# A mixer block on one core: separate first loads, later zeroing, two more tiles finished by accumulating transfers, and a new step list

## The chip, the cores and the metric

The kernel runs on one core of a Trainium2 chip. The core's engines work side by side, each through its own instructions in order: TensorE (PE in the profile; its weight loads are listed as PEld), VectorE (DVE), ScalarE (ACT) and GpSimd (POOL). SyncE (SP) issues most DMA transfers here; ScalarE and POOL issue some as well. The metric is the time of one execution in microseconds (us) on the device. For the kernel before it is 189.82 us, the median of three runs (189.74 to 190.06).

## The reference

The input x has 2048 rows of 512 bfloat16 numbers. After a layer norm, two branches run on the same normalised rows xn: a local attention with 32 heads of 16 numbers, eight positions per row at a distance of 2 (branch A), and a small mixer with two dense stages (branch B). The output is x + A * silu(B).

```python
def _A_ref(x, wqkv, wo):
    q, k, v = ...                    # x @ wqkv, 32 heads of 16
    idx = pos[:, None] - off[None, :]      # off = 0, 2, ..., 14
    logits = jnp.einsum("bhsd,bhswd->bhsw", q, kg) * scale
    logits = jnp.where(mask[None, None, :, :], logits, -1e9)
    attn = _softmax(logits, axis=-1)
    o = jnp.einsum("bhsw,bhswd->bhsd", attn, vg)
    return o @ wo                    # heads put side by side again

def _B_ref(x, w1, w2, w3, w4):
    h = _gelu(_layernorm(x, axis=-1) @ w1)
    # four quarters of h, shifted by +1, -1, +2, -2 rows, then @ w2
    x1 = x + hs
    h2 = _gelu(_layernorm(x1, axis=-1) @ w3) @ w4
    return x1 + h2

xn = _layernorm(x, axis=-1)
s = _A_ref(xn, A_wqkv, A_wo)
g = _silu(_B_ref(xn, B_w1, B_w2, B_w3, B_w4))
return x + s * g
```

## The kernel before

The 2048 rows are four chunks of 512, and a chunk is four tiles of 128 rows, so the tiles are numbered 0 to 15. Row p*4 + i of a chunk stands in partition p of the chunk's tile i. All is computed in bfloat16 with sums in float32.

The kernel is written as some seventy small functions, the steps, each of which emits a few instructions for a tile or a chunk. A long text, ORDER, lists the steps with their arguments, and the instructions of each engine stand in exactly that order: `w1.5.3` is the step w1 for tile 5 with its sums in bank 3. Nothing else schedules the work. An instruction waits where it needs another's result; everything behind it on its engine waits with it. That holds for the transfers that SP issues, too.

The steps that matter here, with the lines of the kernel before:

- Loads. `ldxp` (L221) loads two tiles of x, 256 KB; `ldxc` (L211) a whole chunk; `ldv`, `ldw1`, `ldqk` and others the weights. All are issued on SP.
- Constants. `c_warm` clears a tile for the warm-up products (`warmup`, L321), which multiply zeros while the first loads are under way. `c_elog` and `c_sel` build selection matrices on POOL. `c_zero` (L288 to L290) stores 14 rows of zeros ahead of the rows of v in DRAM, and clears the edges of hT.
- First norm. For chunk 0, `st` (L333) takes the statistics of a tile on VectorE, `sq0` (L338) a root on ScalarE, `nm0` (L345) scales the tile, `tr0` (L356) turns it with four transposes on TensorE, and `ev0h` or `ev0a` take it from PSUM to xnT. Later chunks are turned by DMA (`xT`).
- Products of xn: `v` (L471), with `ev` and `sv` (L489) that store v to DRAM; `qk` (L443); `w1` (L496), with `eh` and the transpose `hTr` (L515).
- Attention: `pw` (L530) multiplies q with k shifted by each of the eight offsets, `lg` (L543) adds up the 16 numbers of a head with 32-column products, softmax follows, `vl` (L710) reads the eight rows of v for a tile from DRAM, `vp` (L716) weights them, `ws` (L729) adds them up on TensorE with 32-column products, `eo` evacuates. The sums are turned by DMA (`oTr`, L748), for the last chunk by TensorE (`oTp`, L756) with `eoT` (L762) on ScalarE to evacuate. `wo` (L768) is the last product of branch A.
- Branch B: `w2` (L611), `xa`, `st3s`, `nm3`, `x1Tr` (L655), `w3` (L668), `eg` (L677), `w4` (L685), `ya` (L692), `si` (L696).
- The end of a tile. For tiles 0 to 11, `sg` (L775) multiplies the sum of `wo` with silu(B) on VectorE, straight from PSUM. The rows of x were copied to the output earlier, from DRAM to DRAM (`pre`, L828, one for each of three chunks), and `soa` (L835) adds the product to them: a transfer with accumulation, issued on POOL. For tiles 12 to 14, `ge` (L782) evacuates the sum on ScalarE, `gb` (L786) multiplies, `fav` (L819) adds x on VectorE, and `so` (L839) stores the tile, on SP for 13 and 14 and on ScalarE's queue for 12. Tile 15 goes in two halves: `woh` (L793), `sgh` (L802), `favh` (L807), `soh` (L813), the first half stored on SP and the second on ScalarE's queue.

Of the kernel before, what the change touches and what calls it, by code (L numbers as in the profile page):

```python
# [22 lines left out]
qk.0.4.1 qk.0.5.5 nmv.6 nmv.7 st.11 ldxc.s.3 st.10 st.8 eqk.0.3 eqk.0.5 qk.0.2.2 eqk.0.0
qk.0.6.4 eqk.0.2 st.9 eqk.0.4 qk.0.7.3 eqk.0.6 eqk.0.7 pw.0.1 rp.5 st.15 st.13 rp.4 xT.3 hTr.0
ldw2.s hTr.1 w1.4.1 v.5.4 ldwo.s.0 ev.5 w1.5.3 v.4.2 ev.4 qk.1.4.4 rs.4 sv.4 v.6.5 w1.7.2 rr.3
rr.2 eh.4 pw.0.2 kh.1 ev.6 sv.5 rs.5 nb.4 pw.0.0 st.12 eqk.1.4 eh.5 w1.6.1 qk.1.1.4 qk.1.2.3
v.7.5 hTr.2 nm.8 nm.9 w2.1.0 pw.0.3 nb.5 rp.6 eh.6 xT.4 vl.s.1.1 eh.7 st.14 rp.7 lg.0.0 rs.7
eqk.1.2 lg.0.1 ev.7 pw.0.5 w2.0.5 rs.6 eqk.1.1 nm.11 nm.10 pw.0.4 sv.7 qk.1.5.4 sv.6 xT.5
qk.1.6.3 xa.1 nb.7 qk.1.0.2 nb.6 st3s.1 eqk.1.6 hTr.3 rr.4 xa.0 ldw3.s.0 st3s.0 eqk.1.5 pw.0.6
nm.13 nm.12 nm.15 qk.1.7.0 qk.1.3.4 w2.2.5 w1.9.3 w1.8.1 eh.9 eh.8 xa.2 rr.7 hTr.4 rr.5 rq.0  # L30
w1.10.5 pw.0.7 r3.0 v.8.3 eh.10 st3s.2 nm.14 w2.3.1 nm3.0 nm3.1 eqk.1.3 w2.5.5 ev.8 qk.2.0.4
xa.3 st3s.3 eqk.1.7 eqk.1.0 xT.6 lg.0.3 rq.1 kh.2 xa.5 lg.0.2 r3.1 w2.4.2 smx.0 ldw3.s.1 sv.8
xT.7 x1Tr.0 v.10.5 qk.2.4.0 w2.6.1 eqk.2.4 nm3.3 xa.4 ex.0 w2.7.3 w1.11.2 xa.6 st3s.6 nm3.2 xa.7
qk.2.5.1 eqk.2.0 x1Tr.1 eh.11 ev.10 sv.10 rr.6 v.9.0 v.11.3 w1.13.4 eqk.2.5 ev.9 hTr.5 qk.2.7.2
w1.15.1 eqk.2.7 w1.12.0 vl.s.2.0 vl.s.0.0 ldw4.s.2 qk.2.2.2 vl.s.3.1 eh.12 pw.1.0 st3s.4 st3s.7
st3s.5 v.12.5 eqk.2.2 pw.1.3 sms.0 eh.13 v.13.0 w3.0.6.4 ev.11 hTr.6 rq.2 qk.2.1.3 pw.1.2 r3.2
sv.9 eg.0.6 eqk.2.1 ldwo.s.3 smn.0 rq.3 pw.1.1 r3.3 w3.0.1.2 qk.2.3.4 w3.0.10.3 nm3.4 eqk.2.3
tE.0 eh.15 eg.0.10 ev.13 eg.0.1 lg.1.1 lg.1.0 pw.1.7 w2.8.1 w1.14.0 w3.0.0.2 eh.14 w3.0.2.3
hTr.7 qk.2.6.0 eqk.2.6 eg.0.0 w2.10.4 nm3.6 vl.s.0.1 nm3.7 x1Tr.3 vl.s.1.0 pw.1.5 xa.8 pw.1.4
nm3.5 pw.1.6 w2.11.1 xa.10 w3.0.8.2 xa.11 qk.3.1.4 st3s.11 eg.0.8 ev.12 w2.14.1 lg.1.2 st3s.10  # L40
sv.12 lg.1.3 eqk.3.1 w2.12.4 sv.11 st3s.8 eg.0.2 smx.1 w2.9.3 ldw4.s.1 x1Tr.2 xa.9 w2.15.5 xa.14
w3.0.3.2 w3.0.9.3 xa.12 pw.2.2 qk.3.2.1 qk.3.0.4 w2.13.0 st3s.9 eqk.3.2 eqk.3.0 eg.0.3 vl.s.9.1
ldw4.s.0 rq.4 xa.15 vl.s.9.0 vl.s.3.0 ldwo.s.2 pre.s.2 qk.3.3.1 w3.0.5.2 st3s.12 qk.3.4.5 eg.0.5
pw.2.3 eqk.3.3 qk.3.5.4 st3s.14 pw.2.4 xa.13 pw.2.1 rq.5 st3s.15 v.15.1 eqk.3.5 v.14.2 ev.15
eqk.3.4 w3.1.1.0 w3.0.4.5 vp.0 st3s.13 rq.6 pw.2.0 r3.4 nm3.9 w3.0.7.1 eg.0.4 ev.14 eg.0.9
eg.0.7 ex.1 qk.3.7.4 w3.1.0.2 eg.1.0 sv.14 r3.5 nm3.10 rq.7 nm3.11 x1Tr.5 w3.1.8.1 vl.s.2.1
pre.s.1 vl.s.10.0 vl.s.10.1 w4.1.3 eqk.3.7 ldwo.s.1 kh.3 sv.15 r3.7 c_sel sms.1 w4.0.5 w4.2.4
ya.0 smn.1 r3.6 w3.1.5.5 w4.3.2 nm3.8 ya.2 ya.1 vp.1 x1Tr.4 w3.1.9.3 nm3.15 eg.1.5 ya.3 w3.1.6.4
pre.s.0 vp.3 tE.1 w3.1.7.2 eg.1.6 eg.1.1 w3.1.3.5 w3.1.4.0 eg.1.7 vp.2 lg.2.1 lg.2.0 qk.3.6.2
eg.1.8 w3.1.10.1 eqk.3.6 nm3.14 pw.2.5 pw.2.7 w3.1.2.4 eg.1.3 eg.1.10 eg.1.4 lg.2.2 pw.2.6  # L50
x1Tr.7 eg.1.2 ws.2.1 ws.1.0 ws.0.4 eg.1.9 pw.3.2 ws.3.3 eo.1 lg.2.3 eo.0 smx.2 vl.s.4.1 w4.6.0
w3.2.0.4 oTr.0 eo.2 eo.3 oTr.1 vl.s.5.1 pw.3.0 ex.2 vl.s.4.0 vl.s.6.0 vl.s.5.0 w4.5.3 vl.s.6.1
ya.6 pw.3.4 w4.7.0 w4.4.1 w3.2.3.5 sms.2 si.2 si.1 si.3 eg.2.0 eg.2.3 si.6 vl.s.7.1 vl.s.7.0
pw.3.1 pw.3.5 nm3.12 ya.4 wo.1.4 nm3.13 ya.7 w3.2.2.1 sg.1 w3.2.9.0 vp.4 ya.5 w3.2.5.4 w3.2.4.5
eg.2.9 w3.2.1.2 smn.2 x1Tr.6 w3.2.8.0 vp.5 eg.2.4 eg.2.2 eg.2.5 w3.2.10.1 w3.2.7.4 w3.2.6.5
eg.2.7 eg.2.10 eg.2.1 eg.2.8 vp.6 tE.2 vl.s.8.1 vl.s.8.0 wo.0.3 eg.2.6 wo.2.1 wo.3.0 pw.3.3 sg.2
w4.10.5 soa.2 sv.13 sg.3 vp.7 w3.3.0.0 lg.3.0 eg.3.0 lg.3.2 si.4 pw.3.6 pw.3.7 ws.4.0 ws.5.1
lg.3.1 ws.7.2 ws.6.4 eo.4 ya.10 lg.3.3 vl.s.11.1 w4.9.0 smx.3 eo.5 si.7 si.0 eo.7 si.5 eo.6
si.10 vl.s.13.1 oTr.2 vl.s.13.0 vl.s.11.0 w4.8.2 vp.9 vl.s.12.1 ex.3 oTr.3 w4.11.4 ya.8 ya.9
sms.3 ya.11 smn.3 w3.3.7.0 w3.3.5.2 w3.3.1.5 eg.3.5 vp.10 tE.3 wo.4.4 eg.3.7 eg.3.1 vl.s.14.1  # L60
vl.s.12.0 sg.0 vl.s.14.0 vp.11 w3.3.4.1 w3.3.9.2 w3.3.10.5 eg.3.10 w3.3.8.0 w3.3.3.3 w3.3.6.5
eg.3.9 eg.3.4 vp.8 w3.3.2.1 eg.3.6 eg.3.8 wo.6.2 eg.3.2 eg.3.3 wo.7.0 sg.6 vp.13 ws.10.3 ws.9.2
eo.10 ws.11.1 ws.8.5 eo.9 w4.13.3 vl.s.15.0 sg.4 vl.s.15.1 vp.12 eo.11 eo.8 wo.5.4 si.11 oTr.5
vp.14 si.9 w4.12.5 oTr.4 w4.15.1 ya.12 sg.5 si.12 si.8 sg.7 vp.15 w4.14.0 soa.1 soa.0 soa.3
# [810 lines left out]
```

## Time and profile before

| | |
|---|---|
| median of the unprofiled runs | 189.82 us |
| the profiled execution | 190.75 us |
| its span, first to last instruction | 189.0 us |
| mean granted TensorE clock | 0.996 |
| TensorE busy | 182.8 us |
| VectorE busy | 165.1 us |
| ScalarE busy | 112.8 us |
| POOL busy | 42.7 us |
| DMA queue of SP, share of 16 engines | 74.6% |
| DMA queue of POOL, share of 16 engines | 10.9% |

The span is measured on the profiled execution from the first to the last instruction, and all moments below count from its start. The profiled execution itself takes 1.75 us more than its span. In the profile, a group of instructions is named by its line and by what it writes and reads (`xr<-mm,xr`); `mm` stands for a bank of PSUM. A matmul's duration there (0.379 us for 512 columns) is longer than the distance from one to the next, since they are pipelined. In the chain of waits the profile goes back from the last instruction, at each step to whatever released it. `xc` is the tile of x, `w2v_sb` holds the weights w2 and wv, `vt` the evacuated sums.

### The profile page before, as it was taken

What the parts mean: (1) busy time and instruction counts of PE and PEld (TensorE: products, weight loads), DVE (VectorE), ACT (ScalarE), POOL (GpSimd) and SP (SyncE); (2) the same over time, 40 slices, a digit from 0 to 9 for tenths busy, and PEclk for the clock granted to TensorE, in tenths of its full rate; (3) what the DMA queues carried; (4) which work ended last, traced back from release to release, by engine and by line L of the source; (5) the groups of instructions that cost most, each with busy time, mean ns of one, the idle gap of its engine ahead of it and who ended that gap; (6) DMA issues with size and microseconds to landing.
All of it is one profiled execution on the core that took longest, in us unless ns stands there. A gap on an engine that the chain in (4) does not pass through costs nothing.

```text
span 189.0 us, 3685 instructions
## 1 busy us (share of the span) xinstructions
PE 182.8 (97%) x1430; PEld 87.0 (46%) x1430; DVE 165.1 (87%) x270; ACT 112.8 (60%) x189; POOL 42.7 (23%) x70
## 2 busy tenths in 40 slices
PE   7999999999999999999999999999999999999990
...
GB/s 164 315 352 115 199 248 141 194 238 137 233 120 286 278 64 224 222 87 190 399 162 361 274 57 134 254 401 277 189 190 95 254 335 238 210 254 106 88 106 116
DMA packets 47842, 39.25 MB, mean 208 GB/s; under 512 B 35251, under 2 KB 41889, under 8 KB 47777
## 3 DMA queue, kind: packets, MB, share of 16 engines
q1 hardware_dynamic: 45008, 35.14, 74.6%
q0 software_dynamic: 2528, 3.69, 10.9%
q8 instruction: 11, 0.18, 0.4%
q10 hardware_dynamic: 288, 0.20, 0.3%
q14 instruction: 7, 0.05, 0.1%
...
## 4 chain that ended last, share of the span: by engine, by line
PE 85%; DMA 4%; DVE 4%; issue 2%; POOL 2%; SPq 1%; ACT 1%; POOLq 0%
PE mm L668 20%; PE mm L685 18%; PE mm L443 15%; PE mm L611 8%; PE mm L496 7%; PE mm L471 6%; PE lg L543 4%; PE mm L768 4%; DMA xc<-in_A_x_dram 3%; PE mm L729 3%; POOL out_dram L835 2%; DMA out_dram<-xr 1%; DVE st L333 1%; DVE xr L775 1%; DVE xr L786 1%
## 5 line engine op out<-in xcount | busy, mean ns | idle before, releaser
L530 DVE TENSOR_TENSOR pw<-qT,kT 128x2048 bf16<-128x2048 bf16 x32 | 38.3, 1214 | 3.4 <-PE lg L543 2.4
L668 PE MATMUL mm<-x1T,w_sb 128*128 128x512 bf16 (+1 forms) x176 | 40.9, 379 | 0.0
L685 PE MATMUL mm<-w_sb,h 128*128 128x512 bf16 (+1 forms) x176 | 39.4, 379 | 0.0
L677 ACT ACTIVATE h<-mm 128x512 bf16<-128x512 f32 (+1 forms) x44 | 23.9, 602 | 23.3 <-PE mm L668 17.6
L716 DVE TENSOR_TENSOR vs<-vs,att 128x4096 bf16<-128x4096 bf16 x16 | 36.2, 2285 | 0.0
L443 PE MATMUL mm<-xnT,wqk_sb 128*128 128x512 bf16 x128 | 30.6, 379 | 0.0
L835 POOL DMA_DIRECT2D out_dram<-xr x12 | 11.0, 1117 | 74.0 <-DVE xr L775 74.0
L668 PEld LDWEIGHTS <-w_sb 128*128 128x128 bf16 (+1 forms) x176 | 17.6, 100 | 20.4
L685 PEld LDWEIGHTS <-h 128*128 128x128 bf16 (+1 forms) x176 | 16.9, 98 | 20.8 <-issue 0.4
L443 PEld LDWEIGHTS <-wqk_sb 128*128 128x128 bf16 x128 | 12.4, 98 | 15.0
L452 ACT ACTIVATE kT<-mm 128x512 bf16<-128x512 f32 x16 | 9.4, 601 | 12.1 <-PE mm L443 11.9
L489 POOL DMA_DIRECT2D v_dram<-vt x16 | 9.6, 601 | 30.6 <-ACT vt L481 27.2
L471 PE MATMUL mm<-w2v_sb,xnT 128*128 128x512 bf16 x64 | 15.8, 379 | 0.0
L496 PE MATMUL mm<-w_sb,xnT 128*128 128x512 bf16 x64 | 15.8, 379 | 0.0
L611 PE MATMUL mm<-w2v_sb,hT 128*128 128x512 bf16 x64 | 15.7, 380 | 0.0
L768 PE MATMUL mm<-wo_sb,oT 128*128 128x512 bf16 x60 | 14.3, 379 | 0.0
L333 DVE BATCH_NORM_STATS2 st<-xc 128x6 f32<-128x512 bf16 x16 | 10.8, 676 | 3.9 <-DMA xc<-in_A_x_dram 3.9
L452 ACT ACTIVATE qT<-mm 128x512 bf16<-128x512 f32 x16 | 9.4, 605 | 7.8 <-PE mm L443 7.7
L635 POOL TENSOR_TENSOR rstd<-nmr,mhalf 128x2 f32<-128x2 f32 x8 | 9.1, 1136 | 19.8 <-DVE nmr L628 19.7
L507 ACT ACTIVATE ht<-mm,rs 128x512 bf16<-128x512 f32 x16 | 10.6, 690 | 4.4 <-PE mm L496 2.3
L696 ACT ACTIVATE xr<-xr 128x512 bf16<-128x512 bf16 x16 | 9.6, 630 | 6.0 <-DVE xr L692 6.0
L692 DVE TENSOR_TENSOR xr<-mm,xr 128x512 bf16<-128x512 f32 x16 | 10.6, 683 | 1.1 <-PE mm L685 0.9
...
## 6 DMA issues: line engine op xcount, KB each, us to landing
...
```

Source lines behind the costliest of these rows:

```text
L443: nc.tensor.matmul(pt, lhsT=wqk_sb[:, dt, nt * P : (nt + 1) * P], rhs=xnT[c][:, :, dt, :], start=(dt == 0), stop=(dt == ND - 1),)
L452: nc.scalar.activation(dst.rearrange("p (n i) -> p n i", i=TPC), mm.pop(("qk", c, nt)).rearrange("p (i n) -> p n i", i=TPC), AF.Copy,)
L471: nc.tensor.matmul(pt, lhsT=xnT[c][:, jj, dt, :], rhs=wv_sb[:, dt, :], start=(dt == 0), stop=(dt == ND - 1),)
L496: nc.tensor.matmul(pt, lhsT=xnT[c][:, jj, dt, :], rhs=w1_sb[:, dt, :], start=(dt == 0), stop=(dt == ND - 1),)
L530: nc.vector.tensor_tensor(out=pw_t[c, u], in0=q_t[c], in1=k_t[c][:, :, DIL * u : DIL * u + CH], op=ALU.mult)
L611: nc.tensor.matmul(pt, lhsT=hT[:, plane, g, p0 : p0 + P], rhs=w2_sb[:, g, :], start=(g == 0), stop=(g == ND - 1),)
L668: nc.tensor.matmul(pt[:fs, :], lhsT=w3_sb[:, dt, ft * P : ft * P + fs], rhs=x1T[c][:, :, dt, :], start=(dt == 0), stop=(dt == ND - 1),)
L677: nc.scalar.activation(h3[c, ft][:fs, :], mm.pop(("w3", c, ft))[:fs, :], AF.Gelu_apprx_tanh)
L685: nc.tensor.matmul(pt, lhsT=h3[c, ft][:fs, jj * P : (jj + 1) * P], rhs=w4_sb[:fs, ft, :], start=(ft == 0), stop=(ft == NF - 1),)
L716: nc.vector.tensor_tensor(out=vv, in0=vv, in1=att[c][:, :, H * jj : H * jj + H].unsqueeze(2).to_broadcast([P, NB * 2, DH, H]), op=ALU.mult,)
L768: nc.tensor.matmul(pt, lhsT=oT[i // 2][:, i % 2, dt, :], rhs=wo_sb[:, dt, :], start=(dt == 0), stop=(dt == ND - 1),)
L835: nc.gpsimd.dma_start(out=rows(out2, i), in_=xr[i], accum_op=ALU.add)
```

## The change

A new step `ldx` loads one tile of x (128 KB), and is used for tiles 0 and 1 in place of one `ldxp`. A new step `preh` copies the rows of x of tiles 12 and 13 to the output, from DRAM to DRAM on SP's queue (256 KB). Tiles 12 and 13 then end like tiles 0 to 11, with `soa` on POOL in place of `fav` and `so`; their product is still `ge` and `gb`. With that, the store of tile 12 on ScalarE's queue and that of tile 13 on SP's queue go away, and one store, the second half of tile 15, stays on ScalarE's queue. `c_zero` and `kh.0` move from the start of the list to behind the first v stores, `c_sel` and `c_elog` to the start. The second warm-up has five products and not eight. The unused step `fag` is dropped. The step list is written anew in full: the same steps otherwise, in another order. Its first and last lines are shown.

```diff
 ORDER = """
-ldxp.s.0 c_warm c_small warmup.10.512.0 sqw c_ident kh.0 ldv.s.0 ldv.s.1 ldxp.s.1 ldw1.s.0
-ldw1.s.1 c_zero st.0 ldxp.s.2 ldxp.s.3 st.1 sq0.0 ldqk.s.0 ldqk.s.1 nm0.0 sq0.1 rp.0 nm0.1
-tr0.0.0 warmup.8.128.1 ev0h.0.0 ev0h.0.1 st.2 tr0.1.2 v.0.1 st.3 ev0h.1.0 ev0h.1.1 sq0.2 v.1.2
-ev.0 nm0.2 sq0.3 rp.1 w1.0.0 ev.1 nm0.3 rs.0 sv.0 st.5 tr0.2.1 ldxc.s.2 w1.1.2 ev0a.2 sv.1 rr.0
-st.4 tr0.3.3 rs.1 v.2.1 ev0a.3 st.7 rp.2 rs.2 w1.2.4 ev.2 st.6 eh.0 v.3.3 sv.2 rp.3 rr.1 w1.3.1
...
-si.14 eo.14 wo.9.3 sg.8 eo.12 eo.13 wo.10.1 soa.8 sg.9 si.15 oTp.13.4 soa.9 sg.10 oTp.14.3
-eoT.13 oTp.12.0 wo.11.5 eoT.12 oTp.15.4 eoT.14 wo.13.0 eoT.15 wo.14.3 wo.12.4 woh.15.0.1
-woh.15.1.2 soa.10 sg.11 soa.11 ge.13 gb.13 ge.14 fav.13 gb.14 so.s.13 ge.12 fav.14 gb.12 so.s.14
-sgh.15.0 fav.12 favh.15.0 so.a.12 sgh.15.1 soh.s.15.0 favh.15.1 soh.a.15.1
+ldx.s.0 ldx.s.1 ldv.s.0 ldv.s.1 ldxp.s.1 c_small sqw c_warm st.0 sq0.0 st.1 nm0.0
+warmup.10.512.0 c_ident c_sel c_elog ldw1.s.0 ldw1.s.1 ldxp.s.2 ldxp.s.3 ldqk.s.0 ldqk.s.1
+tr0.0.1 rp.0 warmup.5.128.0 sq0.1 nm0.1 ev0h.0.0 tr0.1.2 ev0h.0.1 ev0h.1.0 v.0.0 ev0h.1.1 st.2
+v.1.1 st.3 sq0.2 nm0.2 sq0.3 rp.1 nm0.3 st.4 rs.0 st.5 rr.0 w1.0.2 ev.0 sv.0 tr0.2.0 ldxc.s.2
+tr0.3.3 ev0a.2 ldw2.s w1.1.4 ev0a.3 rs.1 v.2.0 rp.2 st.6 v.3.3 rs.2 ev.2 st.7 ev.1 w1.2.5 eh.0
+rr.1 rp.3 sv.1 nmv.5 w1.3.1 rr.2 rs.3 nmv.4 qk.0.2.0 xT.2 sv.2 nmv.6 eh.1 nmv.7 qk.0.0.2 ev.3
+xT.3 eqk.0.2 qk.0.6.4 sv.3 st.11 c_zero st.8 qk.0.5.0 eqk.0.6 ldxc.s.3 eh.3 eqk.0.0 st.9 st.10
+rp.4 qk.0.3.3 hTr.0 qk.0.4.1 eqk.0.3 kh.0 qk.0.1.2 eqk.0.5 eqk.0.4 rs.4 qk.0.7.0 eqk.0.1 w1.5.1
+eqk.0.7 eh.2 pw.0.1 hTr.1 w1.4.2 v.4.5 rp.5 nb.4 nm.9 pw.0.0 rr.3 rs.5 v.5.0 vl.s.0.1 qk.1.0.3
...
+eg.3.10 eg.3.9 ws.8.4 ws.9.2 ws.11.0 ws.10.5 vp.12 w4.14.3 vl.s.15.0 si.11 vl.s.15.1 eo.9 eo.8
+si.9 eo.10 w4.12.4 ya.14 oTr.4 vp.14 sg.7 preh.s eo.11 si.8 si.14 w4.13.0 oTr.5 soa.5 soa.2
+soa.1 soa.6 soa.7 w4.15.1 ya.12 ya.13 vp.15 si.12 si.10 wo.8.0 wo.9.4 sg.8 ya.15 ws.12.3 ws.13.0
+ws.14.1 sg.9 eo.12 si.13 ws.15.4 soa.8 soa.9 eo.14 wo.10.3 si.15 eo.13 oTp.12.1 sg.10 oTp.14.5
+eoT.12 wo.11.2 eo.15 soa.10 oTp.13.1 eoT.14 sg.11 wo.12.3 eoT.13 soa.11 wo.14.2 ge.12 oTp.15.1
+gb.12 ge.14 wo.13.3 soa.12 eoT.15 gb.14 ge.13 fav.14 woh.15.0.1 woh.15.1.2 so.s.14 gb.13
+sgh.15.0 soa.13 favh.15.0 sgh.15.1 soh.s.15.0 favh.15.1 soh.a.15.1
 """
...
     @step
+    def ldx(q, i):
+        if 0 not in x_c:
+            x_c[0] = rot("xc", 0, 2, [P, TPC, D])
+        qs[q].dma_start(out=xtile(i), in_=rows(x2, i))
...
     @step
-    def fag(i):
-        nc.gpsimd.tensor_tensor(out=xr[i], in0=xtile(i), in1=xr[i], op=ALU.add)
...
+    @step
+    def preh(q):
+
+        def half(t):
+            return t[(NCH - 1) * CH :, :].rearrange("(p i) d -> p (i d)", i=TPC)[:, 0 : 2 * D]
+
+        qs[q].dma_start(out=half(out2), in_=half(x2))
```

More of the change, by code (lines that the diff above doesn't have):

```diff
@@ L23 @@
[L23 to L64, printed above, removed]
@@ new lines @@
+rp.4 qk.0.3.3 hTr.0 qk.0.4.1 eqk.0.3 kh.0 qk.0.1.2 eqk.0.5 eqk.0.4 rs.4 qk.0.7.0 eqk.0.1 w1.5.1
+eqk.0.7 eh.2 pw.0.1 hTr.1 w1.4.2 v.4.5 rp.5 nb.4 nm.9 pw.0.0 rr.3 rs.5 v.5.0 vl.s.0.1 qk.1.0.3
+pw.0.2 ev.5 ev.4 qk.1.6.4 pw.0.3 w1.7.5 eqk.1.6 kh.1 sv.4 eh.5 sv.5 v.6.0 eh.4 st.14 qk.1.5.1
+nm.8 hTr.2 st.13 ev.6 w1.6.2 eh.7 st.12 xT.4 eh.6 lg.0.0 lg.0.1 rr.4 st.15 rp.7 qk.1.1.5 sv.6
+pw.0.7 nb.5 hTr.3 w2.1.2 eqk.1.1 rp.6 rs.6 rs.7 nm.10 qk.1.2.0 xa.1 nm.11 w2.0.5 v.7.2 eqk.1.2
+xT.5 st3s.1 pw.0.6 qk.1.3.0 xa.0 w2.2.4 vl.s.1.0 ldw3.s.1 ldw3.s.0 st3s.0 nb.6 rq.0 xa.2 eqk.1.3
@@ new lines @@
+w2.3.5 v.9.0 eqk.1.0 ev.7 nm.13 eqk.1.5 w1.9.4 ev.9 w1.8.1 pw.0.5 xa.3 st3s.3 r3.0 qk.1.4.5
+st3s.2 sv.7 v.8.0 eqk.1.4 rr.5 nb.7 eh.8 rq.1 qk.2.6.2 nm3.1 nm3.0 r3.1 pw.0.4 eh.9 w1.10.1 ev.8
+hTr.4 nm.12 nm3.2 sv.8 sv.9 lg.0.3 lg.0.2 nm3.3 eh.10 qk.1.7.0 eqk.2.6 smx.0 nm.15 w1.11.2 xT.6
+nm.14 w2.4.1 eh.11 x1Tr.1 eqk.1.7 qk.2.2.4 xa.4 v.10.0 pw.1.1 x1Tr.0 w2.5.1 pw.1.3 xT.7 qk.2.3.2
+xa.5 qk.2.4.5 hTr.5 w2.7.1 pw.1.2 st3s.4 eqk.2.2 ev.10 w2.6.0 vl.s.3.0 ex.0 eqk.2.4 rr.6
+vl.s.0.0 w1.13.5 v.11.4 xa.6 st3s.5 qk.2.0.0 vl.s.3.1 xa.7 ev.11 pw.1.0 eqk.2.3 w3.0.6.1 st3s.6
@@ new lines @@
+w1.12.2 rr.7 st3s.7 v.12.4 eh.12 w1.15.3 rq.2 sms.0 r3.2 sv.10 lg.1.0 sv.11 eh.15 lg.1.1 eh.13
+eqk.2.0 hTr.6 w2.9.2 xa.9 smn.0 rq.3 nm3.5 w1.14.5 qk.2.7.0 nm3.4 eh.14 pw.1.5 qk.2.5.2 eqk.2.7
+hTr.7 vl.s.2.0 w2.8.5 pw.1.7 r3.3 w3.0.3.0 ev.12 xa.8 v.13.4 ev.13 eg.0.6 tE.0 sv.12 qk.3.1.3
+w3.0.0.5 eg.0.0 st3s.9 pw.1.4 w3.0.10.1 vl.s.2.1 eg.0.10 pw.1.6 eg.0.3 ldw4.s.2 ldw4.s.0 x1Tr.2
+vl.s.1.1 w2.11.4 ldw4.s.1 eqk.2.5 w2.10.5 xa.11 xa.10 v.15.0 w3.0.7.2 eg.0.7 ev.15 sv.15 kh.2
+st3s.11 w3.0.4.5 w2.12.4 w3.0.8.0 eg.0.8 eqk.3.1 w2.15.2 vp.0 w2.14.1 xa.12 st3s.10 nm3.7
```

24 lines of the change are left out of this document (21 added, 3 removed).

## The prediction

> **What bounds the kernel now.** First the page: its span, the busy times, and TensorE's row of the forty slices (tenths of a slice).
>
> ```profile
> span 189.0 us, 3685 instructions
> ...
> PE 182.8 (97%) x1430; PEld 87.0 (46%) x1430; DVE 165.1 (87%) x270; ACT 112.8 (60%) x189; POOL 42.7 (23%) x70
> ...
> PE   7999999999999999999999999999999999999990
> ```
>
> TensorE is full in all but the first and the last slice. Busy can hide waiting, so next the chain of waits in order of time (start, length, what).
>
> ```profile
> 2.15 5.68 DMA xc<-in_A_x_dram
> 7.83 0.02 issue
> 7.85 0.71 DVE st L333
> ...
> 9.64 0.42 DVE xr L345
> 10.07 0.05 issue
> 10.11 0.40 PE mm L356 x4
> ...
> 15.13 6.91 PE mm L443 x32
> ```
>
> From 10.11 the chain runs on TensorE: 32 products in 6.91 us are 0.216 us each, and the product groups (0.86 us for four) follow each other up to 170.05, with one gap of 0.02. So the middle cannot get faster unless products go away. Only the two ends can: what holds up the products until 10.11, and what follows the last one. What holds them at 10.11 is the second load of x, tiles 2 and 3, issued at 2.15 and landed at 7.83. Its statistics and scaling on VectorE follow (7.85 to 10.05), then the transposes tr0.2.
>
> For the tail I read the timeline (start, length, engine, line) and the table of DMA issues of the last microseconds.
>
> ```profile
> 171.87 2.28 DVE L716 TENSOR_TENSOR vs<-vs,att 128x4096 bf16<-128x4096 bf16 x1
> 172.25 3.51 POOL L835 DMA_DIRECT2D out_dram<-xr  x4 [13.06 <-DVE xr L775]
> ...
> 180.90 1.09 ACT L762 ACTIVATE oT<-mm 128x512 bf16<-128x512 bf16 x2 [0.22 <-PE mm L768]
> 180.90 0.69 DVE L775 TENSOR_TENSOR xr<-mm,xr 128x512 bf16<-128x512 f32 x1 [0.84 <-PE mm L768]
> ...
> 181.88 0.86 POOL L835 DMA_DIRECT2D out_dram<-xr  x1 [0.56 <-DVE xr L775]
> ...
> 183.51 1.04 PE L793 MATMUL mm<-wo_sb,oT 128*128 128x256 bf16 x8
> ...
> 183.71 0.60 ACT L782 ACTIVATE vt<-mm 128x512 bf16<-128x512 f32 x1 [0.27 <-PE mm L768]
> ...
> 186.37 0.34 ACTq L813 DMA_DIRECT2D out_dram<-xr  x1
> ```
>
> Call the start of the half products woh (L793) W: 183.51 here. The last evacuation ge.12 (L782) begins at W + 0.20 and ends at W + 0.80, six VectorE operations then run back to back, the last store is issued at 186.37 (W + 2.86) and lands 1.56 later, at 187.93; the span ends 1.07 after that.
>
> **The change, part by part.** *Products.* Both orders hold the same products, but for three fewer warm-up products of 128 columns (0.056 us each); TensorE waits at that place anyway, so nothing. Stretches with the 32-column products number nine in both, so nothing there.
>
> *First x loads.* Tiles 0 and 1 come in a load each: tile 0 can land earlier than 3.59, by up to about half of the 0.66 us that lie between the landings of 256 KB loads below, and one issue of 0.40 is added on SP's queue ahead of the weights. Neither moves the products: tr0.2 waits for tiles 2 and 3, which stand behind the same bytes as before and are asked for 0.40 later (about 2.55). They landed 5.68 after their issue, and the four 256 KB loads behind them at 8.5, 9.2, 9.8 and 10.5, so the queue, not the issue, set 7.83. I take 7.83 again; bounds: 0.4 later (the issue shows in full) and 1.0 earlier (the first rival).
>
> *tr0.2 and tr0.3.* Before, w1.1 stood between them; now they are neighbours, and w1.1 follows. VectorE scales tile 3 from 10.23 to 10.64, so tr0.3 starts at 10.70 and w1.1 at 10.92 (four transposes at 0.056). Before, both were through at 11.29 + 0.22 = 11.51; now at 10.92 + 0.86 = 11.78. All later products shift by +0.27. Bounds 0 to +0.4.
>
> *Rows zeroed later.* The 14-row store and its memsets (L288: 0.73 of issue, 4.0 to landing; 2 x 0.35; 0.14) move on POOL from 1.3 to 2.8 to behind the fourth v store, which was issued at 15.96. The rows are then there by about 16.5 + 0.73 + 4.0 = 21.3 at the latest. Their reader, the first v load on SP, now stands behind two hT transposes, which were issued at 21.33 and 23.38 (1.34 long): three microseconds of cover. If that goes, SP holds hTr.2, xT.4, hTr.3 and xT.5 behind it, and chunk 1 of the products comes late. The selection constants move to the start of POOL (about 3 us of small operations, done by 5; POOL's next work waited for VectorE until 5.98). Nothing for both.
>
> *The copy preh* is a new SP issue (0.6) and 256 KB from DRAM to DRAM, ahead of oTr.5. Landings around a 512 KB copy were 2.0 us apart (95.07 to 97.07), so half of it puts oTr.5 back by about 1.0 + 0.6. A transpose of o lands 4.4 to 5.6 after its issue, 7.2 in all. Between the sums ws of tile 11 and its reader wo.10 stand four w4 groups (2.38 each), two wo (0.86) and one ws stretch (1.73): 13 us, of which o's evacuation takes some 4. Hidden, with 2 to spare.
>
> *Middle.* The rest of the list is reordered. TensorE had no wait to lose there, so it can only stay or get worse. Bounds 0 to +1.2 (third rival); I take 0.
>
> *woh waits.* Before, the transposes oTp.15 stood three products' groups ahead of woh, and their evacuation eoT.15 was done in time. Now TensorE has wo.14, oTp.15, wo.13, woh, and ScalarE has ge.14, eoT.15, ge.13. Count from the issue s of wo.14's last product. It ends at s + 0.38, ge.14 starts at s + 0.41, eoT.15 0.49 later (two L762 of 0.60 in 1.09) and ends at s + 1.50; woh can start at s + 1.55. TensorE is free at s + 0.22 + 0.22 (oTp.15) + 0.86 (wo.13) = s + 1.30. It waits 0.25. Behind it stand only the eight half products, and with them the end. Bounds +0.15 to +0.4.
>
> *Behind W.* ge.13 starts at W - 0.05 (when wo.13's result is there) and ends at W + 0.55; gb.13 runs from W + 0.59 to W + 1.01. VectorE then has four operations, two additions fewer than before: in the old spacings (0.34, then 0.45, 0.20, 0.45) the last begins at W + 2.03, the ScalarE store is issued 0.37 later and lands 1.56 after that, at W + 3.96, 0.46 earlier than the old W + 4.42. But tile 13 is now added by an accumulating store on POOL. POOL begins 0.29 after VectorE (L775 ends at 181.59, L835 starts at 181.88), at W + 1.30, and such a store landed 2.95 to 3.4 after its start in the last four issues of the table. I take 3.05 (the one at 181.88, with another 1.5 ahead of it, took 3.0): W + 4.35. So the accumulating store becomes the last to land, and the gain of the VectorE chain shrinks from 0.46 to 0.07. Bounds: -0.46 to +0.3.
>
> *Sum.* W moves by 0.27 + 0.25 = +0.52; the last landing by 0.52 - 0.07 = **+0.45 us**. Against the profiled span: 189.0 + 0.45 = 189.45. The profiled execution took 190.75, 1.75 more than its span; the median of the unprofiled runs is 189.82. I put the difference on the median: **190.3 us**, +0.24%.
>
> **Rivals.** *The x load comes early: faster.* If the split loads and the removal of the 14-row store from the first 5 us let tiles 2 and 3 land by 6.8, the products start sooner: the warm-up ends at 5.63 and tr0.0, tr0.1, v.0, v.1 and w1.0 need 3.5 us (0.4, 0.3, 0.2, 1.73 and 0.86 with the warm-ups between), so tr0.2 could come at 9.1 and not 10.11. That is -1.0 on my sum: 189.3. It decides once the landing is 0.85 early. For: the half of wv ahead of this load landed 2.9 after the half before it (4.3 and 7.2), though 256 KB take 0.66, so something held the queues there, and the 14-row store was under way just then (1.50 to 5.50). Against: the bytes ahead are the same.
>
> *The accumulating store hides.* If it lands with the ScalarE store, at W + 3.96, the sum is +0.06: 189.9, no change. For: nothing else loads the queues then. Against: none of twelve landed in under 2.95.
>
> *A wait in the middle.* SP issues in order, and a transpose there took 12.1 us to land (73.39) where 3 to 5 are usual. If such a lag hits a place where the new order has a shorter cover, TensorE waits; a lag 1.2 us beyond the cover gives 191.5. For: transposes and loads are reordered everywhere. Against: the old order stood through such a lag with no wait.
>
> *POOL's store waits for VectorE.* favh.0 and favh.1 (0.28 and 0.29) run while soa.13 is being issued. If POOL stands still under them, the landing is 0.57 later: 190.9. Against: the four stores of 172.25 lie under a VectorE operation on two bf16 tensors that runs from 171.87 to 174.15, and they still took 0.88 each (3.51 for four), like the lone one at 181.88 (0.86). The Trainium skill (SBUF — State Buffer, "SBUF: two separate sides") states the rule behind this rival: GpSimd cannot write the descriptors of its DMAs while VectorE holds the port that the two share. By that rule soa.13 would be late as said; this trace does not show it.
>
> *That the change does nothing* is excluded: all its steps are in the built order.
>
> **How the numbers follow.** Forecast 0.40 (own range 189.9 to 190.8), early x load 0.22, hidden store 0.12, wait in the middle 0.18, POOL behind VectorE 0.08. This kernel's measurement tells about 0.2%, 0.38 us: slower means above 190.2, faster below 189.44. Slower: most of the forecast (0.30), the middle (0.17) and POOL behind VectorE (0.07): 0.54. Faster: most of the early load (0.19), and cases in which half of that comes together with the hidden store (0.05): 0.24. No change: the rest, 0.22. The range reaches from the early load to the wait in the middle, 189.1 to 191.5.
>
> **What would show it.** Right: tr0.3 starts about 0.6 after tr0.2; TensorE waits some 0.25 for the oT evacuation before the half products; the last landing is POOL's store; no other TensorE wait of over 0.1. Wrong: tiles 2 and 3 landing before 7; a gap in the chain between 15 and 175; the ScalarE store last.

## The result, and the profile after

The changed kernel takes 192.56 us, the median of five runs (192.20 to 193.01); the kernel before 189.83 (189.74 to 190.37). The ratio is 1.0131, 95% interval 1.0109 to 1.0154: slower by 2.7 us where the prediction had 0.45. The profiled execution took 192.23 us with a span of 190.4, that is 1.4 more than the span of before; the other 1.3 us are not in this pair of profiles, because the profiled execution of before (190.75) lies 0.9 above the median of its kind and that of the changed kernel 0.3 below its own.

The page of the changed kernel: span, busy times, and TensorE's row of the forty slices.

```profile
span 190.4 us, 3675 instructions
...
PE 182.6 (96%) x1427; PEld 86.3 (45%) x1427; DVE 164.1 (86%) x268; ACT 111.6 (59%) x188; POOL 44.0 (23%) x72
...
PE   7889999999999999999999999999999999999980
```

TensorE is as full as before, so the loss lies at the ends again. First the start, from the timeline of the changed kernel (start, length, engine, line; idle time before and what ended it):

```profile
9.39 0.29 ACT L344 ACTIVATE ve<-mv,eps_t 128x1 f32<-128x1 f32 x1 [0.50 <-DVE rs L350]
9.44 0.41 DVE L351 TENSOR_SCALAR xr<-xc,mv,rs 128x512 bf16<-128x512 bf16 x1
9.59 0.58 ACT L487 ACTIVATE vt<-mm 128x512 bf16<-128x512 f32 x1
...
10.03 0.41 DVE L351 TENSOR_SCALAR xr<-xc,mv,rs 128x512 bf16<-128x512 bf16 x1
10.22 0.68 PE L362 MATMUL mm<-ident,xr 128*128 128x128 bf16 x8 [0.51 <-ACT vt L487]
...
10.73 0.81 PE L502 MATMUL mm<-w_sb,xnT 128*128 128x512 bf16 x3
```

Tile 2 is scaled at 9.85, yet its transposes (L362) start at 10.22: they write PSUM bank 0, which v.0 holds until ScalarE's ev.0 (L487) has emptied it, and ev.0 stands on ScalarE behind the root for tile 3 (L344). This wait costs nothing, though. The eight transposes of L362 are tr0.2 and tr0.3; with the window opened at 10.605 the same view shows the second four alone:

```profile
10.50 0.40 PE L362 MATMUL mm<-ident,xr 128*128 128x128 bf16 x4
```

tr0.3 starts right behind the scaling of its tile (10.03 + 0.41 = 10.44), with or without the bank, and w1.1 (L502) follows it at 10.73. All of that hangs on the load of tiles 2 and 3, landed at 7.62.

The end, from the same timeline:

```profile
182.78 1.03 PE L774 MATMUL mm<-wo_sb,oT 128*128 128x512 bf16 x4
183.25 0.86 POOL L845 DMA_DIRECT2D out_dram<-xr  x1 [0.59 <-DVE xr L792]
183.25 0.59 ACT L768 ACTIVATE oT<-mm 128x512 bf16<-128x512 bf16 x1
...
183.90 1.05 PE L799 MATMUL mm<-wo_sb,oT 128*128 128x256 bf16 x8
...
184.48 0.42 DVE L792 TENSOR_TENSOR xr<-vt,xr 128x512 bf16<-128x512 bf16 x1 [0.20 <-ACT vt L788]
...
185.20 0.86 POOL L845 DMA_DIRECT2D out_dram<-xr  x1 [1.09 <-DVE xr L792]
...
186.30 0.37 ACTq L819 DMA_DIRECT2D out_dram<-xr  x1
```

With W for the start of the half products (L799): W is 183.90, 0.39 later than before. ScalarE's last store goes out at W + 2.40 (before: 2.86), and still the span ends at W + 6.54 (before: 5.46). What follows the last instruction of the work is seen in the view of the program's last line, L880 (number of instructions; shortest, median and longest in ns; first and last start):

```profile
L880 POOLq DRAIN  x3: 40/102/4482, 185.2 to 190.2; - x3
L880 SPq DRAIN  x3: 7/7/13, 189.0 to 189.9; - x3
```

The same view of the kernel before (its last line is L870):

```profile
L870 POOLq DRAIN  x3: 40/102/4267, 181.9 to 188.7; - x3
L870 SPq DRAIN  x3: 7/7/12, 188.1 to 188.5; - x3
```

At the end each engine drains, and all wait for one another. GpSimd's drain begins with its last store and takes over 4 us. Before, it began at 181.9 and was over at 186.13, long before SP was through with its waits for the stores (188.2). Now it begins at 185.2 and is over at 189.66, when SP has been waiting since 189.04. SP itself was through later, too, at W + 5.14 and not W + 4.70: 0.44 of the 1.08 that the tail is longer stand there already, ahead of the drain. SP's waits for the other engines in the last microseconds (total, times, longest) name TensorE's sequencer (PEq), whose signal comes last. In the changed kernel

```profile
SPq L880 <- PEq L880: 1.3, 2, 0.8
```

and before

```profile
SPq L870 <- PEq L870: 0.7, 2, 0.5
```

In both kernels one of the two waits is 0.5 long. The other, which begins when SP is through with the stores, is 0.8 in the changed kernel, where GpSimd's drain is still running, and 0.2 before.

A second effect is in the table of DMA issues, cut to ScalarE's last store (KB, us to landing): in the changed kernel

```profile
out_dram<-xr ACTq DMA_DIRECT2D x1, 64.0 KB, 2.2
```

and 1.6 before. It now moves beside GpSimd's accumulating store and lands at 188.53, 0.19 after it (188.34): the last landing is ScalarE's, and still it is GpSimd's drain that ends last.

### The profile page after: what moved, and what is told of

Read it like the earlier page. It is cut to its first block, busy times and chain, and to the rows that moved or that the text cites. A ratio compares the mean times of both kernels' runs of the same rounds, so it can differ in the third digit from the quotient of the medians.

```text
span 190.4 us, 3675 instructions
## 1 busy us (share of the span) xinstructions
PE 182.6 (96%) x1427; PEld 86.3 (45%) x1427; DVE 164.1 (86%) x268; ACT 111.6 (59%) x188; POOL 44.0 (23%) x72
## 4 chain that ended last, share of the span: by engine, by line
PE 91%; DMA 3%; DVE 2%; ACT 1%; SPq 1%; issue 0%
PE mm L674 20%; PE mm L691 20%; PE mm L449 15%; PE mm L617 7%; PE mm L502 7%; PE mm L774 6%; PE mm L477 6%; PE lg L549 4%; PE mm L735 4%; DMA xc<-in_A_x_dram 3%; DVE st L339 1%; SPq L240 0%; ACT vt L788 0%; SPq L212 0%; DVE xr L808 0%
## 5 line engine op out<-in xcount | busy, mean ns | idle before, releaser
L683 ACT ACTIVATE h<-mm 128x512 bf16<-128x512 f32 (+1 forms) x44 | 24.4, 598 | 18.8 <-PE mm L674 18.7
L845 POOL DMA_DIRECT2D out_dram<-xr x14 | 12.3, 1242 | 59.9 <-DVE xr L781 58.2
L641 POOL TENSOR_TENSOR rstd<-nmr,mhalf 128x2 f32<-128x2 f32 x8 | 8.3, 1044 | 54.0 <-DVE nmr L634 54.0
L502 PE MATMUL mm<-w_sb,xnT 128*128 128x512 bf16 x64 | 16.1, 379 | 0.3 <-DMA w_sb<-in_B_w_dram 0.2
L487 ACT ACTIVATE vt<-mm 128x512 bf16<-128x512 f32 x16 | 9.3, 597 | 6.9 <-issue 5.1
L749 ACT ACTIVATE o<-mm 128x512 bf16<-128x512 f32 x16 | 9.1, 595 | 6.6 <-PE mm L735 6.6
```

The costliest lines, as they stand in the source:

```text
L502: nc.tensor.matmul(pt, lhsT=xnT[c][:, jj, dt, :], rhs=w1_sb[:, dt, :], start=(dt == 0), stop=(dt == ND - 1),)
L683: nc.scalar.activation(h3[c, ft][:fs, :], mm.pop(("w3", c, ft))[:fs, :], AF.Gelu_apprx_tanh)
L845: nc.gpsimd.dma_start(out=rows(out2, i), in_=xr[i], accum_op=ALU.add)
```

## The experiments

Unless said otherwise an experiment changes the step list alone. The table gives for each profile when tiles 2 and 3 of x landed, W, when GpSimd's last store was issued and had landed and its drain was over, when SP's own waits were over, and the end of the span counted from W; then the median and the ratio to the kernel before on the same chip (interval).

| kernel | x landed | W | GpSimd: issued, landed, drained | SP done | end - W | median | ratio |
|---|---|---|---|---|---|---|---|
| before | 7.83 | 183.51 | 181.88, 184.90, 186.13 | 188.21 | 5.46 | 189.83 | |
| b_again | 6.98 | 183.03 | 181.41, 184.65, 185.88 | 187.73 | 5.45 | 190.15 | 1.0006 (0.9991 to 1.0020) |
| after | 7.62 | 183.90 | 185.20, 188.34, 189.66 | 189.04 | 6.54 | 192.56 | 1.0131 (1.0109 to 1.0154) |
| a_again | 8.14 | 184.42 | 185.72, 189.03, 190.35 | 189.73 | 6.71 | 192.29 | 1.0107 (1.0085 to 1.0129) |
| a_oldend | 7.98 | 184.28 | 182.18, 185.28, 186.52 | 188.68 | 5.15 | 190.41 | 1.0015 (0.9993 to 1.0037) |
| a_oldend_2 | 6.66 | 182.94 | 180.84, 184.12, 185.35 | 187.33 | 5.14 | 190.92 | 1.0040 (1.0020 to 1.0059) |
| b_newend | 6.76 | 182.56 | 184.11, 188.14, 189.45 | 188.84 | 7.67 | 191.60 | 1.0082 (1.0054 to 1.0109) |
| a_eot | 7.72 | 183.77 | 185.74, 188.93, 190.24 | 189.62 | 7.24 | 192.45 | 1.0124 (1.0095 to 1.0152) |
| a_soa12 | 8.48 | 184.76 | 184.11, 187.28, 188.56 | 189.15 | 5.15 | 190.41 | 1.0015 (0.9997 to 1.0033) |
| a_plain13 | 7.75 | 184.04 | 185.34, 187.38, 188.70 | 188.33 | 5.43 | 190.36 | 1.0025 (1.0008 to 1.0042) |
| a_ldxp | 6.02 | 182.81 | 184.11, 187.56, 188.87 | 188.25 | 6.83 | 191.62 | 1.0086 (1.0071 to 1.0100) |
| a_ldxp_2 | 6.50 | 182.79 | 184.08, 187.37, 188.68 | 188.06 | 6.66 | 191.57 | 1.0085 (1.0066 to 1.0103) |

**The kernel before again.** Nothing is changed.

> The kernel before once more, unchanged, for a second profile. Its profiled execution shown first (190.75 us, span 189.0) is 0.9 us above the median of its runs (189.83), while the profile of the changed kernel (192.23, span 190.4) is at the low end of its own (192.20 to 193.01). So the two profiles hide 0.9 of the 2.7 us. Theory 1: that first profile was late at its start, tiles 2 and 3 of x landing at 7.83 where other executions get them near 6.9; expected here a span near 188.1, with the half products (L793) starting near 182.6 and the tail as before (5.5 us from there to the end of the span). Rival: the start is the same and that tail was slow; expected the half products again at 183.5 and a tail of 4.6 us.

Measured: span 188.5; tiles 2 and 3 landed at 6.98, W at 183.03, and the tail is 5.45, unchanged. So theory 1 holds in kind: the first profile was late at its start. Half of the 0.9 us came back here, though the landing is 0.85 earlier: the chain of waits now goes back to the first load of x (issued at 0.72), and TensorE no longer waits for tiles 2 and 3. Three more profiles with the single load in the old list (b_newend, and b_best and b_czero below) have W at 182.56 to 182.73, after landings at 6.76 to 6.84.

**The finish of tiles 12 and 13: undone, and alone.** a_oldend:

```diff
-preh.s
...
-gb.12 ge.14 wo.13.3 soa.12
+gb.12 ge.14 wo.13.3 fav.12 so.s.12
...
-sgh.15.0 soa.13 favh.15.0 sgh.15.1
+sgh.15.0 fav.13 favh.15.0 so.a.13 sgh.15.1
```

> The changed kernel with the old finish of tiles 12 and 13 alone: both added on VectorE and stored by SP and by ScalarE, no copy of x into their rows. Theory 1 (the tail): in the profile after, GpSimd's drain, which begins with its last accumulating store, ends at 189.66, 0.62 after SP's last drain (189.04), and that accumulating store lengthened the last ScalarE store from 1.56 to 2.23 us; from the start of the half products to the end of the span it is 6.5 us, before 5.5. Undone, the tail is 5.5 again: 192.56 - 1.05 = 191.5 us. Rival (the end is unimportant, start and middle lose it all): 192.5 us.

b_newend, the list of before:

```diff
+preh.s
...
-gb.13 ge.14 fav.13 gb.14 so.s.13
+gb.13 soa.13 ge.14 gb.14
...
-so.s.14 sgh.15.0 fav.12 favh.15.0 so.a.12
+soa.12 so.s.14 sgh.15.0 favh.15.0
```

> The kernel before with the new finish alone: tiles 12 and 13 as accumulating stores behind their gating, the copy of x into their rows ahead of them, nothing else. Here the accumulating store of tile 12 is GpSimd's last, issued about 1.55 after the start of the half products. Theory 1 (GpSimd's drain after its last accumulating store, 4.46 us from its start in the profile after, sets the end): the span ends 1.55 + 4.46 + 0.78 = 6.8 after the start of the half products, before 5.5: +1.3, 191.1 us. Rival (the accumulating stores cost nothing, the end hangs on the last half store, and VectorE has one addition less ahead of it): 189.4 us.

Measured: undone, 190.41, tail 5.15; alone, 191.60, tail 7.67. Both are on the side of theory 1, and both effects are larger than expected: 2.15 (between two measurements; on one chip it is 1.4, see below) and 1.7 us against 1.05 and 1.3. In b_newend the drain was over 5.34 after the store's issue and not 4.46. The tail is the same sum in every kernel where GpSimd ends last: store issued after W, drain, 0.78 (after: 1.30 + 4.46 + 0.78 = 6.54; b_newend: 1.55 + 5.34 + 0.78 = 7.67).

**Which property of the late store costs.** a_soa12 finishes tile 13 alone in the old way:

```diff
-sgh.15.0 soa.13 favh.15.0 sgh.15.1
+sgh.15.0 fav.13 favh.15.0 so.a.13 sgh.15.1
```

> The changed kernel with tile 13 alone finished in the old way (added on VectorE, stored by ScalarE); tile 12 keeps its accumulating store, and the copy of x into the rows stays. GpSimd's last accumulating store is now that of tile 12, issued 0.65 before the half products, so by a drain of 4.3 to 5.4 us it is through 3.7 to 4.8 after their start, while SP's last wait comes about 5.1 after it. Theory 1 (only an accumulating store that comes late costs): 190.4 us, as with the old finish of both tiles. Rival (each of the two, or the copy of x, costs its share): 191.2 to 191.8 us.

a_plain13 stores tile 13 plainly from GpSimd's queue, and so leaves x out of its rows:

```diff
-soa.13
+so.g.13
```

> The changed kernel with GpSimd's last store a plain one at the same place: the store of tile 13 doesn't accumulate, so x is left out in the rows of tile 13. Theory 1a (GpSimd's queue and its drain cost, whatever the kind of store): the drain again lasts over 4.2 us from the store's start and ends the span, 192.2 to 192.6 us. Theory 1b (the accumulation costs, since the rows are read, added and written back): the store lands about 1.9 after its start, the ScalarE store behind it in 1.56 and not 2.23 to 3.1, the drain lasts about 3.1 and ends before SP's last one; 190.5 us.

Measured: a_soa12 is at 190.41, as with both tiles undone; its accumulating store of tile 12 was drained at 188.56, 0.59 before SP. So an accumulating store in good time costs nothing, nor does the copy preh, which stays here. a_plain13 is at 190.36, theory 1b. Its timeline and its drain:

```profile
185.34 0.57 POOL L848 DMA_DIRECT2D out_dram<-xr  x1 [1.09 <-DVE xr L791]
```

```profile
L879 POOLq DRAIN  x3: 40/93/3381, 185.3 to 189.2; - x3
```

The plain store landed after 2.04 us, the accumulating one after 3.14 to 4.03 at such places, and ScalarE's store behind it after 1.62. The drain still ended 1.32 after the landing and outlasted SP by 0.37: that belongs to GpSimd's queue and leaves a tail of 5.43, near the 5.15 of the old finish. The other 1.1 (6.54 - 5.43) is the accumulation.

**The wait of the half products.** a_eot:

```diff
-ge.12 oTp.15.1 gb.12 ge.14 wo.13.3 soa.12 eoT.15 gb.14
+ge.12 oTp.15.1 eoT.15 gb.12 ge.14 wo.13.3 soa.12 gb.14
```

> The changed kernel with one step moved: the evacuation of the last oT (tile 15) stands ahead of the gating of tile 14 on ScalarE. In the profile after, the half products started at 183.90, 0.26 after TensorE was free. Theory 1: that wait goes and everything behind it comes 0.25 earlier: 192.3 us, half products 0.25 earlier. Rival (the gatings of tiles 14 and 13 come 0.5 later instead and so does VectorE's chain behind them): 192.5 us or more.

Measured: 192.45. The median lies between the two expectations, and the interval overlaps that of the changed kernel; the profile speaks for the rival. TensorE no longer waits (0.22 between the last product of `wo` and the first half product, 0.47 in the changed kernel), but the gating of tile 13 comes later, and with it the accumulating store, from W + 1.30 to W + 1.97, and the tail grows by 0.70.

**The first loads.** a_ldxp, and b_ldx the other way round in the list of before:

```diff
-ldx.s.0 ldx.s.1 ldv.s.0 ldv.s.1 ldxp.s.1
+ldxp.s.0 ldv.s.0 ldv.s.1 ldxp.s.1
```

> The changed kernel with tiles 0 and 1 of x in one load again, nothing else. In the four profiles with the old single load, tiles 2 and 3 were asked for at 2.15 and landed at 7.83, 6.98 and 6.76; with two loads they were asked for at 2.64 and landed at 7.62, 7.72 and 7.98. Theory 2 (the second load's issue of 0.49 puts all later loads back): landing some 0.5 earlier and 192.0 to 192.2 us. Rival (the landing is set by something else, as the prediction had it): 192.5 us.

> The kernel before with tiles 0 and 1 of x in a load each, nothing else. Theory 2 (0.49 of issue ahead of every later load): tiles 2 and 3 land at 7.5 or later, the products start some 0.4 later, 190.3 us. Rival (no effect): 189.9 us.

(The profiles with the single load were three at that time, with the three landings given.) Measured: a_ldxp 191.62, more than theory 2 expected; tiles 2 and 3 landed at 6.02. b_ldx 190.30, ratio 1.0012 (1.0000 to 1.0023); landing at 6.93, W at 182.60. Each of these two profiles is of the fastest execution of its kernel (191.41 and 189.79), so that these landings are early ones of their kind. By the medians the split costs much in the one list and little in the other, and 0.49 of issue ahead of the later loads does not explain both.

**Late zeroing.** b_czero moves `c_zero` behind the fourth v store in the list of before:

```diff
-ldw1.s.1 c_zero st.0
+ldw1.s.1 st.0
...
-sv.3
+sv.3 c_zero
```

a_czero moves `c_zero`, `c_elog` and `c_sel` of the changed kernel back:

```diff
-warmup.10.512.0 c_ident c_sel c_elog ldw1.s.0 ldw1.s.1 ldxp.s.2
+warmup.10.512.0 c_ident ldw1.s.0 ldw1.s.1 c_zero ldxp.s.2
...
-eqk.0.2
+eqk.0.2 c_elog
...
-sv.3 st.11 c_zero st.8
+sv.3 st.11 st.8
...
-sv.14
+sv.14 c_sel
```

> The kernel before with the zeroing of the 14 rows and the halo memsets moved behind the fourth v store, nothing else. Theory (the prediction's first rival: that store, under way from 1.5 to 5.5, holds the queues): tiles 2 and 3 land near 6.0 and not at 6.76 to 7.83, the half products start at 182.5, and the median comes to the low end of the kernel before, 189.7 to 189.8 us. Rival (no effect): landing at 6.8 to 7.8, 189.9 to 190.1 us.

> The changed kernel with the zeroing and the constants back in their old places, the two separate loads of tiles 0 and 1 kept. In five profiles with separate loads and late zeroing, tiles 2 and 3 landed at 7.62 to 8.48; with separate loads and early zeroing (the kernel before with the split alone) at 6.93. Theory (separate loads only hurt where the rows are zeroed late): landing near 7, 191.9 us. Rival (the separate loads hurt by themselves in this list): landing at 7.6 or later, 192.5 us.

Measured: b_czero 189.95, ratio 0.9983 (0.9967 to 0.9999), landing at 6.84, W 182.73: no earlier landing, if anything a small gain. a_czero 191.92, ratio 1.0081 (1.0052 to 1.0110), landing at 6.56, as the theory had it, but in the fastest execution (191.32). One such profile, overlapping intervals and the constants that moved along are not enough to call it shown that separate loads hurt only together with late zeroing.

**Both undone.** a_both is a_oldend and a_ldxp together.

> The changed kernel with both suspects undone: tiles 12 and 13 finished in the old way, no copy of x, and tiles 0 and 1 in one load; the rest of the change (rows zeroed later, constants, new list) stays. Alone, the old finish took 2.15 us off (190.41) and the single load 0.94 (191.62). If the two are independent: 192.56 - 3.1 = 189.5 us, below the kernel before, with tiles 2 and 3 of x landing near 6.0 again. Rival (they overlap, or the new list has a loss of its own): 190.0 us or more.

Measured: 190.23, ratio 0.9990 (0.9972 to 1.0009), where the kernel before took 190.24 on that chip; landing at 6.33, W 183.04, tail 5.21. Nothing of the loss is left, but the two do not add up to 3.1 us.

**The parts on one chip.** The changed kernel and the two undoings again, unaltered.

> The changed kernel once more, unchanged, beside the two undoings on one chip. Theory: the end is the start of the accumulating store of tile 13, 1.3 after the half products, plus a drain of 4.4 to 5.4, plus 0.78: 6.5 to 7.5 from the half products to the end of the span; tiles 2 and 3 land at 7.6 or later and the half products start 76.3 + 100 later, so near 184; 192.5 us. Rival (tiles 2 and 3 land early in half of the executions, as in the kernel before): a profile with the half products near 182.9, and times spread from 191.3 to 193.

> The changed kernel with the old finish of tiles 12 and 13 again, on the chip of a_again. By the spans (6.5 to 6.8 against 5.15 to 5.2) it is 1.4 to 1.6 below a_again; by the medians so far 2.15.

> The changed kernel with tiles 0 and 1 of x in one load again, on the chip of a_again. Theory: tiles 2 and 3 land near 6.0 to 6.4, the half products start near 182.8, 0.9 to 1.1 below a_again. Rival (the 0.94 was the other chip): 0 to 0.4 below.

Measured: kernel before 189.92 (189.72 to 190.45), a_again 192.29 (191.25 to 192.89), a_oldend_2 190.92 (189.85 to 191.44), a_ldxp_2 191.57 (191.22 to 192.27). In a_oldend_2 the times fall into two groups, five from 189.85 to 190.24 and seven from 190.84 to 191.44; its profile is of the first (189.85, landing at 6.66, W 182.94), that of a_oldend of the second (191.20, landing at 7.98, W 184.28). So the load lands early in some executions and over a microsecond later in others, and a median of few runs depends on the mixture. Lowest against lowest and highest against highest the finish costs 191.25 - 189.85 = 1.40 and 192.89 - 191.44 = 1.45, what the tails say (6.5 to 6.8 against 5.15). The single load leaves the lowest time alone (191.22 and 191.25) and takes off the high ones (192.27 and 192.89). Its chain of waits starts differently, too (start, length):

```profile
0.74 2.66 DMA xc<-in_A_x_dram
6.67 1.79 PE mm L476 x8
...
14.09 6.91 PE mm L448 x32
```

The chain goes back to the first load of x, not to that of tiles 2 and 3, and the products of q and k (L448) start at 14.09; at 15.21 in the changed kernel, whose chain begins:

```profile
2.64 4.99 DMA xc<-in_A_x_dram
...
15.21 6.91 PE mm L449 x32
```

**Versions that may beat both.** b_best is the kernel before with two new steps in place of `sgh`: ScalarE copies each half result out of PSUM, VectorE multiplies it as bf16.

```diff
+    def geh(i, h, k):
+        tg[i, h] = rot("vt", k, NVT, [P, D])
+        nc.scalar.activation(tg[i, h][:, 0:DH2], mm.pop(("wo", i, h))[:, 0:DH2], AF.Copy)
...
+    def gbh(i, h):
+        x = xr[i][:, h * DH2 : (h + 1) * DH2]
+        nc.vector.tensor_tensor(out=x, in0=tg.pop((i, h))[:, 0:DH2], in1=x, op=ALU.mult)
```

b_best2 also zeroes the rows late and interleaves VectorE's last operations, and b_best3 asks for tiles 2 and 3 ahead of the second half of wv as well:

```diff
-gb.12 so.s.14 sgh.15.0 fav.12 favh.15.0 so.a.12
-sgh.15.1 soh.s.15.0 favh.15.1 soh.a.15.1
+geh.15.0.16 gb.12 so.s.14 geh.15.1.17 gbh.15.0 fav.12 gbh.15.1
+so.a.12 favh.15.0 soh.s.15.0 favh.15.1 soh.a.15.1
```

> A version that may beat both: the kernel before, with the two half results of tile 15 copied out of PSUM by ScalarE and multiplied by VectorE as bf16, as tiles 12 to 14 are, and with tile 12 added ahead of them. VectorE's last four operations then take the spacing of its bf16 ones (0.2 to 0.35) and not 0.45 after each PSUM one. Theory: the last store is issued about 2.4 after the start of the half products and not 2.86; 189.5 us. Rival (ScalarE's copies, which stand behind the one of tile 12 and wait for the second half products until 1.25 after the start of the first, take the place of VectorE's chain): 189.9 us.

> The kernel before with the rows zeroed later (0.17% faster alone, interval 0.01 to 0.33%) and with the last six VectorE operations interleaved: both half results come through ScalarE, and no operation follows the one that makes its input (in b_best such pairs started 0.32 to 0.47 apart, others 0.21). Expected: last store issued 2.45 after the start of the half products, not 2.81 to 2.86; the end 5.05 after it, not 5.4; 0.4 us below the kernel before, 189.5 us. Rival (a wait for ScalarE's second copy takes the gain): 2.8 again and 189.9 us.

> b_best2 with the load of tiles 2 and 3 issued ahead of the second half of wv. Theory (the landing of tiles 2 and 3 makes the spread): it lands near 5.8, the half of wv near 6.6, just as the first v product needs it (6.58 in b_best2); spread of the times below 0.4 us, median 189.5. Rival (the first v product now waits for that half of wv): products 0.3 to 0.8 later, 190.0 us.

> b_best2 unchanged, beside b_best3 on one chip: 0.15 to 0.4 us below the kernel before (189.5 to 189.8 us); rival: no difference.

Measured: b_best 190.16, ratio 0.9995 (0.9975 to 1.0015); the last store left at W + 2.81, since three of VectorE's last operations follow right behind the one that feeds them and start 0.32 to 0.47 after it. b_best2 189.76, ratio 0.9989 (0.9977 to 1.0001), and on another chip 189.71, 0.9986 (0.9977 to 0.9995): the second interval is below one. The medians lie 0.16 and 0.35 us under the kernel before; the tail is 0.31 shorter (5.15 against 5.46 in both profiles). What the later zeroing adds to that is not shown. Its timeline, with W at 182.53:

```profile
183.36 0.43 DVE L791 TENSOR_TENSOR xr<-vt,xr 128x512 bf16<-128x512 bf16 x1
183.70 0.28 DVE L817 TENSOR_TENSOR xr<-vt,xr 128x256 bf16<-128x256 bf16 x1
183.90 0.42 DVE L834 TENSOR_TENSOR xr<-xc,xr 128x512 bf16<-128x512 bf16 x1
184.24 0.28 DVE L817 TENSOR_TENSOR xr<-vt,xr 128x256 bf16<-128x256 bf16 x1
...
184.44 0.48 DVE L822 TENSOR_TENSOR xr<-xc,xr 128x256 bf16<-128x256 bf16 x2
...
184.96 0.34 ACTq L828 DMA_DIRECT2D out_dram<-xr  x1
```

The last store leaves at W + 2.43, as expected, and the span ends at W + 5.15, not 5.05: that store took 1.69 to land. b_best3 189.96, ratio 0.9993 (0.9980 to 1.0006), spread 0.60: the theory fails. The load of tiles 2 and 3, now third, landed at 6.70, 2.3 after the one ahead of it, and the half of wv at 7.40: the delay stays, and here it hits what is third.

## Why the prediction was right and wrong

- **Behind W, -0.07: the step that failed.** VectorE's chain came as predicted: soa.13 was issued at W + 1.30 and ScalarE's store at W + 2.40, and soa.13 landed at W + 4.44 (4.35 predicted). What failed is the way from the landings to the end. "The span ends 1.07 after that" was read off a store of ScalarE (1.03 by the unrounded span), and the prediction moved the end of the span with the last landing alone, also when that was to be GpSimd's. From GpSimd's landing to the end it is 1.32 + 0.78 = 2.10. With this the same sum gives W + 6.45; measured 6.54. The profile of before held it: its GpSimd drain ended 1.23 after the landing, hidden under SP's last waits. A second price was wrong as well: ScalarE's store, taken at 1.56, needed 2.23 beside the accumulating one and landed at W + 4.63, not W + 3.96. So the last landing was ScalarE's, which the prediction had named as a sign of being wrong; it did not set the end. The runs put the whole finish at 1.4 us.
- **First x loads, nothing.** "They landed 5.68 after their issue ... I take 7.83 again" took one execution for the rule. With the old list the landing was at 6.53 to 7.83 in seven profiles with the single load, and 7.83 is the latest; with the changed list and two loads it was at 7.62 to 8.48 in six of seven and at 6.66 in one. So the base was late by chance, and the prediction, which put its +0.45 on the better median, missed that the changed kernel is late as a rule: of its eleven executions in two measurements one took 191.25 us, and the others 191.78 to 193.01. On one chip the two loads cost 0.72 in the median.
- **tr0.2 and tr0.3, +0.27: right.** From the landing of tiles 2 and 3 to W it is 175.68 in the profile of before and 176.28 in that of the changed kernel, 0.60 more. Up to the products of q and k it is 7.30 and 7.59 (15.13 - 7.83, 15.21 - 7.62), and these 0.29 are this term: w1.1 waits for tr0.3 and tr0.3 for the scaling of tile 3, 3.11 from the landing to w1.1 where the prediction had 3.09. Only its sign did not show: tr0.3 started 0.28 after tr0.2 and not 0.6, since tr0.2 waited for bank 0 of PSUM, which the prediction had not looked at and which cost nothing.
- **woh waits, 0.25: right.** 0.47 against 0.22 is 0.25. W itself moved by 0.39 in this pair of profiles, and not by 0.52, because the landing of tiles 2 and 3 was 0.21 earlier than in the late one of before. That it gains nothing to take the wait away (a_eot) was not foreseen.
- **Rows zeroed later, preh, middle: right as far as seen.** b_czero is no slower; whether the later zeroing costs something beside the two loads stays open (a_czero). a_soa12, which keeps preh, equals a_oldend, which drops it; from the first products of q and k to W it is 168.38 before and 168.69 after, 0.06 more beyond that wait.
- **The rivals.** *The early x load* was seen where the prediction didn't look: with the single load kept and the rows zeroed late (a_ldxp, a_ldxp_2, a_both) tiles 2 and 3 landed at 6.02 to 6.50, but W stayed at 182.8 to 183.0: the chain of waits goes back to the first load of x there, and the change as made has two loads. *The accumulating store hides* fell: its landing and the drain behind it set the end. *GpSimd's store waits for VectorE* fell: soa.13 took 0.86 to issue with favh.0 under way, as the others. The prediction had stretched the rule of the Trainium skill (SBUF — State Buffer, "SBUF: two separate sides"): the same section reports that VectorE operations on two tensors, which favh.0 is, were not seen to stall GpSimd's DMAs, and the trace agrees. *A wait in the middle* did not come.
- **The sum.** Lowest times on one chip: 191.25 - 189.72 = 1.53, of which 1.40 is the finish. The medians differ by 2.37; the rest, some 0.8, is put down to the late landing, which comes more often with the changed start. What makes one early load land 1.1 to 2.9 us after the one ahead of it, where the next ones follow in some 0.7, stays open, and so does why the changed start meets it more often.
